# A new written-out order for an attention-plus-MLP kernel: 128 product sets instead of 137, and loads placed anew

## The chip, the cores and the metric

The kernel runs on one core of a Trainium2 chip. The metric is the device time of one execution in microseconds; runs are compared by their median.

## The reference, cut to what matters

Four batches of q, k and v, each 6080 x 256. Over the 6080 rows, the columns of q and k are normalised; the 256 x 256 scores go through a softmax; v is multiplied by the result; and the 24320 rows that come out go through a two-layer MLP with a tanh gelu and 2048 hidden units.

```python
qn = q / (np.linalg.norm(q, axis=1, keepdims=True) + 1e-06)
kn = k / (np.linalg.norm(k, axis=1, keepdims=True) + 1e-06)
s = kn.transpose(0, 2, 1) @ qn / tau          # 256 x 256 for each batch
a = np.exp(s - s.max(-1, keepdims=True))
a /= a.sum(-1, keepdims=True) + 1e-09
x = (v @ a).reshape(B * S, D)
h = x @ w_in
g = 0.5 * h * (1.0 + np.tanh(c * (h + 0.044715 * h * h * h)))
return g @ w_out
```

## The kernel before

**Stages.** The attention matrix is multiplied into `w_in` once for each batch (steps `aw.*`, `ac.*`), so the rest works directly on v. The 24320 tokens are cut into 25 blocks, mostly of 1024 tokens, six to a batch and seven in the last; a block is two halves of up to 512 tokens. Batch 0's scores are made first, from q and k in one go. The scores of batches 1, 2 and 3 are made in small pieces between the blocks of the batch before.

**A block's first product.** The hidden units are cut into 16 chunks of 128. A plain step `g.u` makes chunk u for both halves with 4 matmuls on TensorE (PE) into a pair of PSUM banks, and `G.u` is its gelu on ScalarE (ACT). A *set* i makes chunks i and 8+i together, in Strassen's manner (Winograd's form): 7 matmuls `m1.i` to `m7.i` instead of 8, on sums of weights (`SW`, tile `sw`) and of tokens (`vs`, tile `tv`, on VectorE, DVE), and in exchange copies and additions: on ACT `wcq` (L613), `wy5` (L616) and three gelus `wGq` (L626), `wGr` and `wGx` (L637), on DVE `wap` (L618) and `wax` (L621). `e` and `E` are block 0's product and gelu in another cut.

**The second product** goes in the same manner: `T1` to `T4` are sums on DVE (L704), `M1` to `M7` the matmuls, `y5`, `cq`, `ap`, `ax` the copies and additions. `c11` to `c22` transpose the result on DVE (L744) into one of three output buffers `ot`, and when a buffer is full four DMAs store it: from SP's queue, and for the last block but one two from SP's and two from POOL's. The last block uses `D` steps.

**Preparation.** `pA21`, `pA12`, `pNA` (ACT) and `pA11`, `pF0`, `pS3` and so on (DVE) make the eight forms of `w_out` from its float32 load `wst`.

**Loads.** `lq.c:b` and `lk.c:b` load a piece of q or k (384 KB, cast to bf16 on the way) from POOL's queue. `lv.h:n` casts half a block of v into bf16 in HBM, also from POOL's queue, and `lt.h:n` is a transposing load of it from SP's queue into `vT`, which has two buffers. POOL's loads wait for the last matmul that was recorded before them; `lt` has no such gate, it waits for its data, its buffer and the entries of SP's queue ahead of it:

```python
def load_vt(n, h):
    x, y = parts_of(n)[h]
    nc.sync.dma_start_transpose(out=vt_tile(n)[:, :, x:y], in_=v_bf.pop((n, h))[: y - x, :])
...
            elif what in ("lq", "lk"):
                load_one(n, *a, "qk".index(what[1]), GATE[0])
            elif what == "lv":
                cast_v(n, *a, GATE[0])
            elif what == "lt":
                load_vt(n, *a)
```

`qsq.c:b` and `ksq.c:b` square a piece (ACT at L158, or DVE at L160 for every other k), `f1` to `f3` fold the squares, `sp` and `sa` sum them, and `row.c_r:b` multiplies 128 of its rows into the 256 x 256 scores (L205). Of a piece, the square or the first `row` is the first use. `pow`, `kf`, `kr`, `krp`, `S`, `th`, `dn`, `rc`, `eT`, `rsum`, `rs` turn the scores into the softmax.

**The order.** Nothing is scheduled automatically. All work from the first `e` on is a string, `ORDER`, of some 3500 words, each `what.arguments@banks:block or batch`. They are recorded one after the other, and each engine runs its instructions in just this order, waiting at each one by semaphore for its inputs and for a free bank or buffer. PSUM banks are named by letters: `h` and `b` are the two pairs, `a`, `s`, `p`, `r` single banks; `m5.1:2` with `@b` means pair b.

```python
        for word in ORDER.split():
            run(word)
```

Of the kernel before, what the change touches and what calls it, by code (L numbers as in the profile page):

```python
# [954 lines left out]
row.0_0@r:1 m1.1@p:1 g.0@b:1 row.0_2@r:1 E.7_1:0 vs:1 lq.2:1 m5.1@h:1 M5.0@a:0 qsq.0:1 wcq.1:1 G.0:1
m6.1:1 f1.0:1 e.7_0@b:0 wy5.1:1 lk.2:1 wap.1:1 m2.1:1 row.0_5@r:1 row.0_4@r:1 row.0_3@r:1 m7.1:1
pA21:0 f2.0:1 SW.1:0 m3.1:1 E.7_0:0 y5:0 wGq.1:1 wax.1:1 g.8@b:1 row.1_4@r:1 T3.0:0 f3.0:1 lv.0:2
row.1_2@r:1 cq:0 m4.1:1 g.10@h:1 wGr.1:1 row.1_3@r:1 row.1_1@r:1 G.8:1 sp.0@p:1 lv.1:2 pS2:0 T2.0:0
T2.1:0 sa.0:1 M2.1:0 M2.0:0 ksq.1:1 qsq.1:1 g.2@b:1 G.10:1 f1.1:1 c11:0 lk.3:1 M6.0:0 f2.1:1
m1.5@p:1 M6.1:0 m5.5@h:1 ap:0 row.1_0@r:1 wcq.5:1 f3.1:1 G.2:1 wy5.5:1 lq.3:1 m2.5:1 m6.5:1  # L960
row.1_5@r:1 T3.1:0 wap.5:1 gc:1 g.3@b:1 M3.1:0 sp.1@r:1 ksq.2:1 lk.4:1 G.3:1 M7.0:0 m3.5:1 M3.0:0
g.11@b:1 T4.0:0 lt.1:2 qsq.2:1 wGq.5:1 lt.0:2 g.12@h:1 f1.2:1 sa.1:1 f2.2:1 M7.1:0 f3.2:1 c12:0
sp.2@r:1 ax:0 wGx.1:1 m7.5:1 G.11:1 m1.6@s:1 sa.2:1 wax.5:1 T4.1:0 G.12:1 g.4@b:1 row.2_1@r:1 lq.4:1
M4.0:0 T1.0:1 m5.6@h:1 row.3_2@r:1 row.3_4@r:1 qsq.3:1 wcq.6:1 G.4:1 m6.6:1 g.7@b:1 wy5.6:1 M4.1:0
wap.6:1 ksq.3:1 lq.5:1 row.3_5@r:1 T2.0:1 wGx.5:1 G.7:1 m4.5:1 m3.6:1 m2.6:1 m7.6:1 row.2_2@r:1
g.15@b:1 f1.3:1 f2.3:1 wax.6:1 wGq.6:1 wGr.5:1 lv.0:3 f3.3:1 c21:0 row.3_0@r:1 row.2_0@r:1 m4.6:1
G.15:1 sp.3@p:1 row.2_5@r:1 row.2_3@r:1 sa.3:1 vs:2 row.2_4@r:1 qsq.4:1 row.3_1@r:1 m1.1@a:2 g.0@h:2
m5.1@b:2 row.3_3@r:1 wcq.1:2 M1.1@p:1 lk.5:1 G.0:2 wy5.1:2 ksq.4:1 m6.1:2 T1.1:1 m2.1:2 wap.1:2
f1.4:1 g.3@h:2 wGx.6:1 wGr.6:1 m3.1:2 m7.1:2 M5.1@s:1 G.3:2 wax.1:2 f2.4:1 lk.6:1 g.8@h:2 f3.4:1
gc:1 wGq.1:2 T2.1:1 m4.1:2 M5.0@s:1 sp.4@r:1 M1.0@p:1 wGx.1:2 lv.1:3 G.8:2 y5:1 m5.2@b:2 sa.4:1  # L970
m1.2@r:2 c22:0 wGr.1:2 T3.0:1 cq:1 m1.5@a:2 m5.5@h:2 wcq.2:2 M2.1:1 m6.2:2 wcq.5:2 M2.0:1 m2.2:2
m6.5:2 wy5.2:2 wy5.5:2 ksq.5:1 T4.1:1 m2.5:2 wap.2:2 c11:1 wap.5:2 m3.2:2 lq.6:1 m7.2:2 wax.2:2
T4.0:1 M6.1:1 M6.0:1 m3.5:2 m4.2:2 wGq.2:2 qsq.5:1 lv.0:4 wGr.2:2 wGq.5:2 g.11@b:2 ap:1 m7.5:2
wGx.2:2 T3.1:1 wax.5:2 f1.5:1 M7.0:1 m1.6@r:2 M7.1:1 m5.6@h:2 G.11:2 lt.0:3 ax:1 f2.5:1 f3.5:1
m4.5:2 g.4@b:2 wcq.6:2 m6.6:2 wGr.5:2 M3.0:1 wy5.6:2 wGx.5:2 sp.5@a:1 M3.1:1 wap.6:2 sa.5:1 G.4:2
m1.7@a:2 m5.7@b:2 m7.6:2 qsq.6:1 ksq.6:1 M4.0:1 m3.6:2 m2.6:2 wcq.7:2 m6.7:2 wy5.7:2 lt.1:3 wax.6:2
m4.6:2 M4.1:1 wGq.6:2 wGx.6:2 f1.6:1 wap.7:2 lq.7:1 m7.7:2 m3.7:2 m2.7:2 f2.6:1 c12:1 g.12@h:2
wax.7:2 wGr.6:2 m1.1@p:3 wGq.7:2 c21:1 T1.0:2 wGx.7:2 row.5_3@r:1 G.12:2 m4.7:2 g.0@b:3 f3.6:1 vs:3
row.5_2@r:1 row.5_0@r:1 row.5_1@r:1 row.5_5@r:1 row.4_2@r:1 row.4_1@r:1 row.5_4@r:1 row.4_4@r:1
m5.1@h:3 wcq.1:3 m1.2@s:3 wGr.7:2 T1.1:2 row.4_3@r:1 G.0:3 sp.6@a:1 m6.1:3 wy5.1:3 m2.1:3  # L980
row.4_5@r:1 wap.1:3 m5.2@b:3 wcq.2:3 lk.7:1 m6.2:3 row.4_0@r:1 sa.6:1 qsq.7:1 m7.1:3 wy5.2:3
M5.1@a:2 m2.2:3 m3.1:3 wax.1:3 gc:1 m4.1:3 M5.0@a:2 wap.2:3 wGx.1:3 wGq.1:3 wGr.1:3 m1.3@r:3 m3.2:3
T3.0:2 m7.2:3 m5.3@h:3 wax.2:3 c22:1 T2.0:2 y5:2 wcq.3:3 wGq.2:3 M1.0@p:2 M1.1@p:2 m6.3:3 wy5.3:3
m4.2:3 T2.1:2 g.8@b:3 m2.3:3 wap.3:3 cq:2 M2.0:2 M2.1:2 ksq.7:1 lv.1:4 wGr.2:3 m3.3:3 m1.5@s:3
# [5 lines left out]
M4.1:2 g.0@h:4 m7.7:3 row.6_2@r:1 m3.7:3 c21:2 m2.7:3 row.7_3@r:1 G.0:4 m1.1@a:4 wax.7:3 m4.7:3  # L990
M3.1:2 M3.0:2 lq.0:2 lv.1:5 wGq.7:3 T1.0:3 vs:4 m5.1@h:4 wGr.7:3 wcq.1:4 c12:2 wy5.1:4 m1.2@s:4
m6.1:4 row.6_5@r:1 m2.1:4 m5.2@b:4 row.7_2@r:1 wap.1:4 wcq.2:4 T1.1:3 m1.3@p:4 row.6_1@r:1 m6.2:4
wGx.7:3 wy5.2:4 wap.2:4 m3.1:4 row.7_1@r:1 m2.2:4 m7.1:4 row.7_5@r:1 wGq.1:4 row.6_4@r:1 wax.1:4
m3.2:4 m7.2:4 row.6_0@r:1 row.7_0@r:1 row.6_3@r:1 row.7_4@r:1 m5.3@h:4 wcq.3:4 T2.1:3 wGq.2:4
wGx.1:4 m4.1:4 m6.3:4 gc:1 m5.4@b:4 m2.3:4 wy5.3:4 wGr.1:4 M5.0@r:3 wax.2:4 wap.3:4 m1.4@a:4 wy5.4:4
# [6 lines left out]
wax.6:4 M3.0:3 m5.7@h:4 m4.6:4 rc.0:1 ax:3 rc.3:1 wGq.6:4 wcq.7:4 c22:3 wGr.6:4 wy5.7:4 M4.0:3
m6.7:4 wap.7:4 M4.1:3 m2.7:4 lv.0:7 wGx.6:4 lq.1:2 m3.7:4 eT:1 m7.7:4 g.0@b:5 c21:3 wax.7:4 wGq.7:4
T1.1:4 G.0:5 rsum@a:1 aw.1@r:1 m4.7:4 g.4@h:5 vs:5 rs:1 M3.1:3 g.8@b:5 c12:3 G.4:5 wGr.7:4 T1.0:4
ac.1:1 m1.1@a:5 m5.1@h:5 aw.0@p:1 wcq.1:5 G.8:5 M5.1@s:4 aw.4@r:1 m6.1:5 wy5.1:5 wGx.7:4 ac.0:1
m2.1:5 m5.2@b:5 m1.2@p:5 wap.1:5 ac.4:1 M5.0@s:4 T2.1:4 m7.1:5 lk.1:2 m3.1:5 lv.1:7 wcq.2:5 y5:4
wy5.2:5 wGq.1:5 wax.1:5 m6.2:5 T3.1:4 M1.1@r:4 m4.1:5 wGr.1:5 M1.0@r:4 m2.2:5 lt.0:6 cq:4 wGx.1:5
wap.2:5 aw.5@a:1 T3.0:4 m7.2:5 g.12@h:5 m3.2:5 T2.0:4 wax.2:5 ac.5:1 wGq.2:5 lt.1:6 M2.1:4 m1.3@a:5
M2.0:4 m4.2:5 m5.3@b:5 wcq.3:5 wy5.3:5 wGx.2:5 wGr.2:5 G.12:5 T4.1:4 m6.3:5 M6.1:4 M6.0:4 c11:4
ksq.0:2 aw.2@p:1 wap.3:5 m7.3:5 m3.3:5 m2.3:5 ap:4 wax.3:5 M7.0:4 m5.5@h:5 ac.2:1 wGq.3:5 m4.3:5  # L1010
m1.5@p:5 M3.0:4 m5.6@b:5 wy5.5:5 wcq.5:5 M3.1:4 m6.5:5 lv.0:8 qsq.0:2 M7.1:4 wGr.3:5 SW.0:1 T4.0:4
c12:4 m1.6@a:5 wap.5:5 aw.3@r:1 ax:4 ac.3:1 wGx.3:5 wcq.6:5 m7.5:5 m3.5:5 m2.5:5 wGq.5:5 M4.0:4
f1.0:2 wy5.6:5 m6.6:5 wax.5:5 wap.6:5 m1.7@r:5 m5.7@h:5 M4.1:4 m2.6:5 m4.5:5 c21:4 m7.6:5 wcq.7:5
# [266 lines left out]
```

## Time and profile before

| | |
|---|---|
| median of three runs | 690.52 us (687.57 to 697.32) |
| the profiled execution's own time | 687.86 us |
| its span, first to last instruction | 686.1 us |
| mean granted TensorE clock | 0.999 |
| busy: PE, DVE, ACT | 97%, 92%, 91% of the span |
| matmuls | 3584 in the trace |
| DMA | 78.80 MB, mean 115 GB/s |
| transposing loads of v | 45, median 5.3 us from issue to landing, 3.1 to 12.4 |
| loads of k and of q (384 KB) | 21 each, median 5.6 and 5.2 us |

Busy times are unions of what an engine's instructions cover; matmuls overlap in them. "Idle before" is the time in which an engine had nothing to do, with the instruction or the DMA whose end released it. The chain of waits starts at the last instruction and goes back, at each step, to what released it.

### The profile page before, as it was taken

To read this page: it belongs to the slowest core of one execution; us is meant where nothing else is said; L and a number is where in the kernel's file an instruction comes from. 1 tells how busy PE (TensorE), PEld (TensorE's weight loads), DVE (VectorE), ACT (ScalarE), POOL (GpSimd) and SP (SyncE) were. 2 spreads that over 40 slices of the span, in tenths; PEclk is the share of its full clock that TensorE was granted. 3 is DMA by queue.
4 is the path that set the end of the run, shared out by engine and by line. 5 is a ranking of instruction groups with operands and counts; after the bars stand their busy time and mean duration, and the time that the engine had idled before them with its cause. 6 is when DMAs were issued, how large, how long until landed. Compare 5 with 4: busy or idle time off the path is not lost.

```text
span 686.1 us, 10286 instructions
## 1 busy us (share of the span) xinstructions
PE 665.7 (97%) x3584; PEld 337.1 (49%) x3584; DVE 629.1 (92%) x938; ACT 621.9 (91%) x941; POOL 74.2 (11%) x137
## 2 busy tenths in 40 slices
...
GB/s 240 207 251 158 124 171 114 102 143 74 142 103 118 167 114 98 100 96 93 103 105 142 142 157 138 84 53 108 79 135 62 91 75 61 72 83 90 76 32 89
DMA packets 161508, 78.80 MB, mean 115 GB/s; under 512 B 148512, under 2 KB 152224, under 8 KB 160736
## 3 DMA queue, kind: packets, MB, share of 16 engines
...
## 4 chain that ended last, share of the span: by engine, by line
PE 85%; DMA 7%; issue 4%; ACT 2%; POOL 1%; DVE 0%; DVEq 0%; POOLq 0%; ACTq 0%
PE p L482 22%; PE r L482 17%; PE rb L482 16%; PE qp L482 12%; PE h L482 10%; PE G L205 4%; DMA qk_g1b<-in_k_dram 3%; PE awp L374 2%; DMA qk_g1a<-in_q_dram 1%; DMA k<-in_k_dram 1%; DMA q<-in_q_dram 1%; ACT g L516 1%; PE e L482 1%; ACT g L637 0%; ACT qp L613 0%
## 5 line engine op out<-in xcount | busy, mean ns | idle before, releaser
L482 PEld LDWEIGHTS <-wcomb 128*128 128x128 bf16 x1408 | 136.5, 98 | 144.5 <-issue 1.7
L482 PE MATMUL p<-t,wcomb 128*128 128x512 bf16 (+2 forms) x576 | 142.8, 373 | 0.1
L482 PE MATMUL r<-g,wcomb 128*128 128x512 bf16 (+2 forms) x576 | 141.8, 373 | 0.0
L626 ACT ACTIVATE g<-qp 128x1024 bf16<-128x1024 f32 (+1 forms) x130 | 132.0, 1022 | 6.1 <-PE qp L482 5.9
L482 PEld LDWEIGHTS <-aw 128*128 128x128 bf16 x872 | 84.8, 98 | 94.8 <-issue 6.3
L704 DVE TENSOR_TENSOR t<-g,t 128x2048 bf16<-128x2048 bf16 (+2 forms) x96 | 112.8, 1182 | 0.0
L482 PE MATMUL rb<-tv,sw 128*128 128x512 bf16 (+3 forms) x288 | 101.4, 366 | 0.1
L618 DVE TENSOR_TENSOR qp<-rb,yw 128x512 f32<-128x512 f32 (+2 forms) x137 | 93.1, 686 | 8.7 <-ACT yw L616 4.8
L621 DVE TENSOR_TENSOR xw<-rb,yw 128x512 f32<-128x512 f32 (+2 forms) x137 | 92.6, 676 | 7.1 <-ACT g L637 3.4
L516 ACT ACTIVATE g<-h 128x1024 bf16<-128x1024 f32 (+1 forms) x92 | 94.1, 1032 | 1.8 <-PE h L482 1.4
L482 PE MATMUL h<-vT,aw 128*128 128x512 bf16 (+2 forms) x376 | 95.0, 377 | 0.6 <-ACT g L516 0.5
L616 ACT ACTIVATE yw<-qp 128x512 f32<-128x512 f32 (+2 forms) x137 | 80.8, 601 | 5.8 <-PE qp L482 4.1
L613 ACT ACTIVATE qp<-rb 128x512 f32<-128x512 f32 (+2 forms) x137 | 80.8, 595 | 4.7 <-PE rb L482 3.4
L637 ACT ACTIVATE g<-xw 128x512 bf16<-128x512 f32 (+1 forms) x130 | 82.1, 635 | 2.2 <-DVE xw L621 2.2
L482 PEld LDWEIGHTS <-sw 128*128 128x128 bf16 x576 | 56.2, 98 | 56.6 <-issue 0.6
L637 ACT ACTIVATE g<-rb 128x512 bf16<-128x512 f32 (+1 forms) x130 | 77.6, 602 | 1.9 <-PE rb L482 1.8
L704 DVE TENSOR_TENSOR t<-g 128x2048 bf16<-128x2048 bf16 (+2 forms) x48 | 56.5, 1181 | 0.7 <-ACT g L626 0.4
L704 DVE TENSOR_TENSOR g<-g,g 128x2048 bf16<-128x2048 bf16 (+2 forms) x48 | 56.6, 1183 | 0.0
L442 POOL DMA_DIRECT2D vb<-in_v_dram x45 | 22.5, 501 | 312.1 <-PE rb L482 199.4
L482 PE MATMUL rb<-tv,aw 128*128 128x512 bf16 (+3 forms) x144 | 50.9, 366 | 2.5 <-DVE xw L621 2.5
L482 PE MATMUL rb<-vT,aw 128*128 128x512 bf16 (+3 forms) x144 | 51.3, 366 | 0.0
L482 PE MATMUL qp<-vT,aw 128*128 128x512 bf16 (+3 forms) x144 | 51.3, 366 | 0.0
...
## 6 DMA issues: line engine op xcount, KB each, us to landing
out_dram<-ot SPq DMA_DIRECT2D x160, 128.0 KB, 3.1
...
```

The source lines that it names most:

```text
L205: nc.tensor.matmul(G[b][:, jc, :], lhsT=qt[:np_, r, jc * 128 : jc * 128 + 128], rhs=kt[:np_, r, :], start=first and jc == 0, stop=jc == 1, ...
L374: nc.tensor.matmul(ps, lhsT=ET[b][:, jc, ic * 128 : ic * 128 + 128], rhs=win_bf[:, jc, fs * 512 : fs * 512 + 512], start=jc == 0, stop=jc ...
L442: after(nc.gpsimd.dma_start(out=vb[: y - x, :], in_=v[b, t0 + x : t0 + y, :]), gate)
L482: GATE[0] = nc.tensor.matmul(*a, skip_group_check=True, **kw)
L516: nc.scalar.activation(g_half(n, u // 8)[:, u % 8].rearrange("p (t x) -> p t x", t=2), hp[:, :, :hc], AF.Gelu_apprx_tanh)
L613: apart(n, i, 0, "act", nc.scalar.activation(QP[n, i][:, 0, :w], RB[n, i][:, :w], AF.Copy))
L616: apart(n, i, 1, "act", nc.scalar.activation(YW[n, i][:, :w], QP[n, i][:, 1, :w], AF.Copy))
L618: apart(n, i, 1, "dve", nc.vector.tensor_add(QP[n, i][:, 1, :w], RB[n, i][:, :w], YW[n, i][:, :w]))
L621: nc.vector.tensor_add(XW[n, i][:, :w], RB[n, i][:, :w], YW.pop((n, i))[:, :w])
L626: nc.scalar.activation(g[:, k0].rearrange("p (t x) -> p t x", t=2), qp[:, :, :hc], AF.Gelu_apprx_tanh)
L637: nc.scalar.activation(g[:, k0, t], x[:, :w], AF.Gelu_apprx_tanh)
L704: nc.vector.tensor_sub(o, a, b)
```

## The change

Only `ORDER` changes. The functions, the tiles, the buffers and the steps before the first `e` are the same.

- Nine blocks have one set less and two plain steps more: blocks 3, 5, 9, 11, 15 and 17 have 5 sets and 6 plain steps (before: 6 and 4), blocks 4, 10 and 16 have 6 and 4 (before: 7 and 2). In all there are 128 sets and 112 plain steps, before 137 and 94.
- Every other step is there as before, and nearly all stand in another place. The words below show the start, the places around batch 3's last loads, and the end.

```diff
-e.0_0@h:0 aw.3@s:0 ac.3:0 aw.2@a:0 e.1_0@b:0 vp.1@r:0 ac.2:0 E.0_0:0 e.2_0@h:0 aw.4@p:0 E.1_0:0
-e.3_0@b:0 lv.1:1 lk.0:1 E.2_0:0 aw.5@s:0 vc.1_0:0 vc.1_1:0 E.3_0:0 e.3_1@h:0 aw.6@a:0 E.3_1:0
-e.0_1@b:0 E.0_1:0 ac.4:0 e.2_1@h:0 ac.5:0 SW.0:0 aw.7@r:0 pA11:0 e.1_1@b:0 E.2_1:0 ac.7:0 e.5_1@h:0
-vp.0@p:1 lq.0:1 E.1_1:0 E.5_1:0 e.4_1@b:0 T1.1:0 pF0:0 pS3:0 e.5_0@h:0 pA12:0 vc.0_1:1 ac.6:0
-E.4_1:0 M1.0@s:0 pF1:0 vc.0_0:1 e.4_0@b:0 lt.1:1 pS1:0 E.5_0:0 e.6_1@h:0 lq.1:1 pNA:0 E.4_0:0
...
-m4.6:14 lk.7:3 wGq.7:14 wax.7:14 m1.2@a:15 row.5_4@s:3 T1.0:14 g.0@b:15 m4.7:14 wGr.6:14 G.0:15
...
-m6.2:15 gc:3 wy5.1:15 wy5.2:15 wGx.7:14 wap.1:15 ksq.7:3 M5.1@p:14 m7.1:15 wap.2:15 wax.1:15
...
-m3.3:24 wGq.3:24 wGx.2:24 wGx.1:24 m7.3:24 D.2_1@r:24 D.2_0@s:24 D.6_0@s:24 D.0_0@s:24 c21:23 c22:23
...
+e.0_0@h:0 aw.3@s:0 aw.2@a:0 e.1_0@b:0 vp.1@r:0 E.0_0:0 E.1_0:0 lk.0:1 ac.2:0 aw.5@p:0 aw.4@a:0
+ac.3:0 e.2_0@h:0 vc.1_0:0 vc.1_1:0 e.2_1@b:0 E.2_0:0 lv.1:1 aw.6@s:0 e.3_0@h:0 aw.7@r:0 ac.4:0
+ac.5:0 E.2_1:0 pA21:0 E.3_0:0 e.3_1@b:0 SW.0:0 E.3_1:0 ac.6:0 e.0_1@h:0 E.0_1:0 e.1_1@b:0 vp.0@a:1
+E.1_1:0 ac.7:0 SW.1:0 lq.0:1 e.7_1@h:0 E.7_1:0 pS3:0 pF0:0 pA11:0 e.5_0@b:0 E.5_0:0 vc.0_0:1
+e.4_0@h:0 lt.1:1 m1.1@p:1 e.6_0@b:0 M1.0@s:0 E.4_0:0 lq.1:1 e.4_1@h:0 M1.1@s:0 pA12:0 E.6_0:0
...
+m1.7@r:14 G.4:14 ksq.6:3 m5.7@b:14 wGx.5:14 wap.6:14 wcq.7:14 wy5.7:14 lk.7:3 T1.0:14 row.4_4@s:3
...
+G.3:15 M2.1:14 wGx.1:15 ksq.7:3 T3.1:14 wap.2:15 M2.0:14 m4.1:15 m3.2:15 wGr.1:15 m7.2:15 g.11@b:15
...
+M3.0:23 M3.1:23 T4.1:23 m6.3:24 M4.0:23 M4.1:23 m2.3:24 D.5_1@a:24 wap.3:24 c21:23 m7.3:24 G.4:24
...
+D.5_0@r:24 D.6_0@r:24 D.2_1@a:24 c12:23 c22:23 D.7_0@r:24 D.3_0@r:24 D.3_1@a:24 D.4_1@a:24
...
```

More of the change, by code (lines that the diff above doesn't have):

```diff
@@ L955 @@
[L955 to L984, printed above, removed]
@@ L990 @@
[L990 to L995, printed above, removed]
@@ L1002 @@
[L1002 to L1013, printed above, removed]
@@ new lines @@
+lv.0:3 wGq.5:1 M7.1:0 M3.1:0 m4.5:1 m5.6@h:1 f1.2:1 wcq.6:1 m2.6:1 f2.2:1 G.15:1 m6.6:1 f3.2:1 ax:0
+c12:0 lq.4:1 wy5.6:1 M4.1:0 wap.6:1 sp.2@s:1 wGr.5:1 wGx.5:1 sa.2:1 M4.0:0 T1.0:1 m3.6:1 m7.6:1
+ksq.3:1 lk.4:1 wax.6:1 T2.0:1 g.7@b:1 wGq.6:1 G.7:1 qsq.3:1 row.3_3@p:1 m4.6:1 row.3_1@p:1
+row.2_2@p:1 row.3_5@p:1 g.4@h:1 row.3_4@p:1 row.3_2@p:1 row.2_1@p:1 m1.1@s:2 g.0@b:2 c21:0
+row.2_3@p:1 row.2_5@p:1 row.2_0@p:1 G.4:1 vs:2 lq.5:1 m5.1@h:2 wcq.1:2 G.0:2 wGr.6:1 wy5.1:2 f1.3:1
+f2.3:1 wGx.6:1 row.3_0@p:1 m2.1:2 T1.1:1 f3.3:1 row.2_4@p:1 m6.1:2 g.8@b:2 gc:1 sp.3@a:1 G.8:2
@@ new lines @@
+m6.2:4 m2.2:4 wax.1:4 wGr.7:3 wap.2:4 row.7_3@a:1 m4.1:4 M5.1@s:3 c22:2 m7.2:4 m3.2:4 gc:1 kf:1
+M5.0@s:3 m1.3@a:4 lv.0:7 wGq.1:4 wGx.1:4 wGr.1:4 wax.2:4 g.8@b:4 wGq.2:4 T2.0:3 m5.3@h:4 m4.2:4 y5:3
+wcq.3:4 m6.3:4 T3.0:3 M1.0@p:3 M1.1@p:3 wGx.2:4 wy5.3:4 wap.3:4 G.8:4 wGr.2:4 m3.3:4 m5.5@b:4 T2.1:3
+m7.3:4 m1.5@r:4 m2.3:4 cq:3 M6.0:3 kr:1 wcq.5:4 wax.3:4 m4.3:4 T4.1:3 m6.5:4 wy5.5:4 M2.1:3 m2.5:4
+wap.5:4 m3.5:4 wGr.3:4 krp@a:1 T4.0:3 S.1:1 T3.1:3 wGq.3:4 S.0:1 g.12@h:4 m7.5:4 M2.0:3 wGq.5:4
+wGx.3:4 G.12:4 wax.5:4 c11:3 M6.1:3 m1.6@a:4 lt.0:5 lt.1:5 ap:3 th.1:1 m5.6@b:4 th.0:1 m4.5:4 dn:1
@@ new lines @@
+m7.2:6 wGq.2:6 wGr.1:6 wGx.1:6 G.3:6 m1.5@r:6 M6.1:5 m5.5@b:6 wcq.5:6 wax.2:6 ap:5 wy5.5:6 g.11@h:6
+lk.4:2 G.11:6 m6.5:6 m4.2:6 wGx.2:6 wGr.2:6 wap.5:6 m2.5:6 c22:4 M3.1:5 m3.5:6 f2.0:2 m7.5:6
+m5.6@h:6 M7.1:5 wax.5:6 T4.1:5 wGq.5:6 m4.5:6 m1.6@s:6 g.4@b:6 f3.0:2 wy5.6:6 M3.0:5 wGr.5:6 wcq.6:6
+wGx.5:6 m1.7@r:6 lq.3:2 lv.0:9 m6.6:6 T4.0:5 G.4:6 c12:5 M7.0:5 sp.0@a:2 m5.7@b:6 wap.6:6 wcq.7:6
+wy5.7:6 m7.6:6 m6.7:6 m2.6:6 qsq.1:2 sa.0:2 row.1_4@a:2 m3.6:6 ax:5 wap.7:6 wax.6:6 M4.1:5 M4.0:5
+row.0_1@a:2 m7.7:6 row.1_3@a:2 row.0_0@a:2 c22:5 row.0_2@a:2 wGx.6:6 wGq.6:6 c21:5 wax.7:6 T1.0:6
@@ new lines @@
+f3.2:2 wGx.1:7 wy5.2:7 G.3:7 T3.0:6 sp.2@s:2 m6.2:7 sa.2:2 M2.1:6 wap.2:7 M6.1:6 c11:6 ap:6 m1.5@s:7
+m5.5@h:7 m3.2:7 m2.2:7 lt.0:8 m7.2:7 M3.1:6 T4.0:6 ksq.3:2 lt.1:8 lv.1:9 M7.0:6 wy5.5:7 lk.5:2
+wGq.2:7 wax.2:7 T3.1:6 wcq.5:7 qsq.3:2 g.11@b:7 M3.0:6 m6.5:7 T4.1:6 m4.2:7 M7.1:6 m2.5:7 c12:6
+G.11:7 wGx.2:7 wap.5:7 m1.6@r:7 wGr.2:7 m5.6@b:7 wcq.6:7 m3.5:7 ax:6 f1.3:2 wGq.5:7 m7.5:7 M4.0:6
+m1.7@a:7 m6.6:7 wy5.6:7 wax.5:7 wGx.5:7 g.4@h:7 lq.5:2 m4.5:7 G.4:7 wGr.5:7 lv.0:10 wap.6:7 f2.3:2
+f3.3:2 m2.6:7 m7.6:7 M4.1:6 T1.0:7 m5.7@h:7 m3.6:7 wax.6:7 wcq.7:7 c21:6 row.2_0@s:2 row.2_1@s:2
@@ new lines @@
+lt.0:9 wGr.1:8 m5.2@h:8 wcq.2:8 wGq.1:8 sp.4@r:2 M6.0:7 wy5.2:8 sa.4:2 c11:7 m6.2:8 qsq.5:2 wap.2:8
+M6.1:7 m1.5@r:8 m2.2:8 m3.2:8 m7.2:8 ap:7 m5.5@b:8 T4.0:7 wcq.5:8 wGq.2:8 M3.0:7 wy5.5:8 ksq.5:2
+m2.5:8 M3.1:7 g.11@h:8 m6.5:8 wax.2:8 lq.7:2 c22:6 c12:7 M7.1:7 m4.2:8 wGx.2:8 G.11:8 wap.5:8 f1.5:2
+wGr.2:8 m7.5:8 m1.6@p:8 m3.5:8 wax.5:8 f2.5:2 f3.5:2 m5.6@h:8 M7.0:7 wcq.6:8 wGq.5:8 m6.6:8 m4.5:8
+m2.6:8 wy5.6:8 ax:7 wGr.5:8 T4.1:7 row.5_3@s:2 g.4@b:8 wap.6:8 row.4_4@s:2 sp.5@r:2 wGx.5:8 sa.5:2
```

488 lines of the change are left out of this document (249 added, 239 removed).

## The prediction

> **What bounds the kernel now.** I read the page first, for the engine that is never free.
>
> ```profile
> PE 665.7 (97%) x3584; PEld 337.1 (49%) x3584; DVE 629.1 (92%) x938; ACT 621.9 (91%) x941; POOL 74.2 (11%) x137
> L626 ACT ACTIVATE g<-qp 128x1024 bf16<-128x1024 f32 (+1 forms) x130 | 132.0, 1022 | 6.1 <-PE qp L482 5.9
> L618 DVE TENSOR_TENSOR qp<-rb,yw 128x512 f32<-128x512 f32 (+2 forms) x137 | 93.1, 686 | 8.7 <-ACT yw L616 4.8
> L621 DVE TENSOR_TENSOR xw<-rb,yw 128x512 f32<-128x512 f32 (+2 forms) x137 | 92.6, 676 | 7.1 <-ACT g L637 3.4
> L516 ACT ACTIVATE g<-h 128x1024 bf16<-128x1024 f32 (+1 forms) x92 | 94.1, 1032 | 1.8 <-PE h L482 1.4
> L616 ACT ACTIVATE yw<-qp 128x512 f32<-128x512 f32 (+2 forms) x137 | 80.8, 601 | 5.8 <-PE qp L482 4.1
> L613 ACT ACTIVATE qp<-rb 128x512 f32<-128x512 f32 (+2 forms) x137 | 80.8, 595 | 4.7 <-PE rb L482 3.4
> L637 ACT ACTIVATE g<-xw 128x512 bf16<-128x512 f32 (+1 forms) x130 | 82.1, 635 | 2.2 <-DVE xw L621 2.2
> L637 ACT ACTIVATE g<-rb 128x512 bf16<-128x512 f32 (+1 forms) x130 | 77.6, 602 | 1.9 <-PE rb L482 1.8
> ```
>
> A busy matmul is drawn 373 ns long but they overlap, so 97% alone proves little. In the trace I took the time from one matmul's start to the next: 216 ns is the middle value for 512 columns, 202 for 480, 109 for 256, 96 for 224. The program's matmuls at these intervals come to 656.6 us. The first starts at 7.0 us and the last at 680.8, so PE stands still for about 17 us between, some 10 of them before 37 us, while the first q and k stream in (both orders have the same steps there). From the first `e` step (37.9 us) to the end only 7.2 us are lost. PE is the bound; DVE and ACT follow within 9%, but nearly never hold it up.
>
> Where those 7.2 us lie, the timeline around the largest tells (start, length, engine, line, and in brackets the idle time before), and then the chain of waits over the same window:
>
> ```profile
> 438.94 1.47 SPq L447 DMA_TRANSPOSE vT<-vb  x1
> 439.30 0.56 POOL L103 DMA_DIRECT2D k<-in_k_dram  x1 [6.66 <-PE rb L482]
> 448.36 1.58 ACT L158 ACTIVATE sq<-k 128x1280 bf16<-128x1280 bf16 x2 [2.90 <-DMA k<-in_k_dram]
> 450.48 0.69 DVE L621 TENSOR_TENSOR xw<-rb,yw 128x512 f32<-128x512 f32 x1 [2.62 <-ACT g L637]
> 451.23 0.38 PE L482 MATMUL rb<-tv,aw 128*128 128x512 bf16 x1 [2.49 <-DVE xw L621]
> ```
>
> ```profile
> 439.30 9.03 DMA k<-in_k_dram
> ```
>
> A transposing load of v goes out, a load of k 0.4 us after it; the k lands 9.03 us later. ACT stands at `ksq.7:3`, whose k is not there; the gelus queued behind it come late, DVE's add behind them, and PE misses its bank: 2.92 us in all (2.66 and 0.27). The same happened near 79 us: a q issued at 71.01 among two transposing loads landed after 7.71 us, and PE lost 0.67 and 0.26 us. So **3.9 us come from loads that land late**. Of the rest, 1.6 us are built in (float32 products of `krp`, 64-row pieces of `row`) or too small to place, and 1.7 us are short waits in crowded places, 0.53 of them at the first `e`, the other 1.2 for ACT.
>
> Of the 48 large q and k loads after 40 us, 24 had no transposing load in flight: they landed after 4.1 to 7.4 us, median 5.0. The other 24 took 4.3 to 12.4, and all nine above 7.4 are theirs.
>
> **The change, part by part.**
>
> *Nine sets become eighteen plain steps.* A set has 7 products, the two `g` steps 8. Six sets are in blocks of 512 columns a half, three of 480: 6 x 0.216 + 3 x 0.202 = 1.90 us; with two tiny filling products PE's sum is 658.5. **+1.9 us**, wholly on the bound engine. What goes away hides behind PE: on ACT 9 x (595 + 601 + 1022 + 602 + 635 - 2 x 1032) ns = 12.5 us, on DVE 9 x (686 + 676) = 12.3 us. I cost this relief at 0, because ACT and DVE already keep up; without that cover it would be the gain. It can loosen the crowded places by up to those 1.2 us.
>
> *Loads and their first uses.* PE is saturated, so a place in its order is a time: I added the intervals up from the first `e` in both orders and noted where each load's releasing matmul and its first reader stand. In the old order the distance is 5.8 us for `lq.7:1`, 6.1 for `lk.7:1`, 6.5 for `lq.7:3`, 6.1 for `lk.7:3`, 6.8 to 8.1 for five more: under the slow landings of 7.4 to 12.4 us. In the new order, from 58 us on, the shortest is 10.1 (`lk.3:1`); `lk.7:3` has 15.6. A transposing load starts when the buffer of two blocks earlier is free and the stores ahead of it on SP's queue are out; placing these the same way, from 58 us on none is issued within 2 us before a q or k load, and each has 10 us or more to its first reader. Even a 9.0 us landing is covered. **-3.9 us**; bounds 0 (the loads find something else to wait for) and -5.1 (the 1.2 us of waits for ACT go too).
>
> Against this stands the Trainium skill (DMA: Bandwidth & Descriptors, section Rules for kernel authors): it says that a transpose beside ordinary DMAs needs nothing, and its section on queues, rings and completion order that each DMA engine takes its queues in turns, a packet at a time. By that, moving them apart would be worth 0, and only the longer distances would help; the sum stays, since they cover the slow landings too. The trace's 12.4 against 7.4 us does not agree that company is free, though it can't tell sharing from blocking.
>
> *The first stage.* New here: `pA21` (1.07 us on ACT) stands ahead of `E.3_0`, and `aw.5`, `aw.4` ahead of `e.2_0`. In this stage PE needs a bank per `e` (0.86 us) and ACT frees it with a gelu each 0.92 to 1.0 us; old ACT had gaps of 0.3 us between them. Following the banks `h` and `b` by hand, `e.0_1` waits 0.7 to 0.95 us for `E.3_0`, and smaller waits follow: 1.2 to 2.0 us late by `g.0:1`, against 0.4 for the old order. **+1.0 us**; bounds 0 (the gaps absorb it) and +2.0.
>
> ```profile
> 42.02 1.02 ACT L536 ACTIVATE g<-e 128x1024 bf16<-128x1024 f32 x1 [0.29 <-PE e L482]
> 43.57 0.54 POOL L442 DMA_DIRECT2D vb<-in_v_dram  x1 [5.49 <-PE e L482]
> 44.10 0.58 POOL L103 DMA_DIRECT2D k<-in_k_dram  x1
> 49.97 1.32 SPq L447 DMA_TRANSPOSE vT<-vb  x1
> ```
>
> Also `lk.0:1` now precedes `lv.1:1` on POOL's queue. The two landed at 49.95 (v) and 51.78 (k); swapped, v lands near 51.8, its transposing load (5.0 us) near 56.8, not 54.97. `vs:1` stands at 55.2, so DVE waits some 1.5 us, which its 8% of idle time absorbs; `g.0:1`, the first matmul that reads it, stands at 57.4 plus the lateness of 1 us, 1.6 us behind the landing. Cost 0, with little cover.
>
> *The tail.* The last transposes to the output wait for a buffer that POOL's stores still read:
>
> ```profile
> 675.87 0.63 POOL L757 DMA_DIRECT2D out_dram<-ot  x1 [53.84 <-DVE ot L744]
> 677.03 4.00 PE L482 MATMUL o<-g,wcomb 128*128 128x224 bf16 x40
> 679.23 1.76 POOL L757 DMA_DIRECT2D out_dram<-ot  x3 [2.74 <-issue]
> 681.65 0.72 DVE L744 STREAM_TRANSPOSE ot<-o 128x224 f32<-128x224 f32 x2 [1.40 <-DMA out_dram<-ot]
> ```
>
> The step that fills that buffer, `c21:23`, moves from 5.9 to 6.8 us ahead of PE's end, so its stores end 1 us earlier: **-1.0 us** of the 1.4; bounds 0 and -1.4. `c22:23` moves later, but its stores have 5 us left.
>
> *Sum.* 686.1 + 1.9 - 3.9 + 1.0 - 1.0 = 684.1 us of span; with the 1.8 us around it in the profiled execution (687.9 - 686.1), 685.9. The three runs shown had a median of 690.5, 2.7 above the profiled execution. If that excess is loads landing later still, the new distances swallow most of it; I keep a quarter, 0.6: **686.5 us**.
>
> **The rivals.**
>
> *The load waits stay.* The distance was not the cause, or a queue slips: POOL issues loads in order, and one waiting for its buffer holds all behind. Then 685.9 + 3.9 = 689.8. Against it: at 448 us the landing and ACT's start are 0.03 us apart. The Trainium skill's rule, if it held alone, would lead here only as far as the distances fail.
>
> *Slower, by the first stage.* DMA is busiest there (the page's DMA digits are 9 in each of the first four slices), so a landing there slips easily. If block 1's transposed half lands 5 us later than I place it, 1.6 us of cover leave 3.4 us of PE wait; with the gelu chain at its upper bound (+1.0), 685.9 + 4.4 = 690.3, slower than the 687.9 it is compared with. It decides from a slip of 3.6 us on (1.6 of cover and the 2.0 by which I forecast less than before). Against it: the old load of the same kind landed in 5.0 us.
>
> *More goes.* ACT's relief removes the crowded waits, the tail wait goes whole and the first stage costs nothing: 686.1 + 1.9 - 5.1 - 1.4 + 1.8 = 683.3.
>
> *The order doesn't keep them apart.* PE's lateness shifts matmul-released loads but not those held by buffers; if pairs meet, a 9 to 12 us landing still fits into distances of 10 to 15 us nearly everywhere: within 1 us of the forecast, so no separate time.
>
> **How the numbers follow.** Forecast 60% (the case of meeting pairs included), load waits stay 18%, first stage slower 13%, more goes 9%. Range 682.5 to 693.5: below, the best case less 0.8; above, the slower rival's 690.3 with the 2.7 us by which the shown median lies over its profile, and 0.5 for late landings. A measurement here tells about 2% (13.8 us) from no change, as the runs from 687.6 to 697.3 suggest; every case lies within that. For faster by more, 676.7, PE would have to lose nothing and start earlier: 1%. For slower by more, 704, an unforeseen wait of 18 us: 3%.
>
> **What would show it.** Right: PE with 3592 matmuls and no wait over 1 us after 60 us; no `sq<-k` on ACT that waits for a DMA; ACT near 610 and DVE near 617 us busy; the last transposes not waiting on `out_dram`. The first-stage step is right if an `e` matmul waits for `g L536` near 46 us. Wrong: a wait of over 2 us on PE behind `sq` or `tv`, or a k or q load that lands after more than 8 us with its reader waiting.

## The result, and the profile after

The changed kernel takes 686.82 us (median of 22 runs, 686.43 to 686.91), the kernel before 690.30 us in the runs beside it (22 runs, 687.57 to 697.32): a ratio of 0.9939, 95% interval 0.9924 to 0.9955. That is 3.5 us less, and within the 2% of "no change". The profiled execution took 686.74 us with a span of 685.0, so between the two profiled executions only 1.1 us lie; the other 2.4 us of the median come from the runs of before, which spread over 10 us and lie, all but two, above their profile, while those of after lie within 0.5 us.

The page of the changed kernel: its engines, two groups that have fewer members now (130 and 137 before) and the plain gelu's, which has more (92 before), each with count, busy us, mean ns, and idle us before with what ended it:

```profile
PE 666.7 (97%) x3595; PEld 337.9 (49%) x3595; DVE 621.2 (91%) x920; ACT 613.8 (90%) x914; POOL 74.2 (11%) x137
...
L626 ACT ACTIVATE g<-qp 128x1024 bf16<-128x1024 f32 (+1 forms) x121 | 122.3, 1021 | 6.3 <-PE qp L482 5.6
L516 ACT ACTIVATE g<-h 128x1024 bf16<-128x1024 f32 (+1 forms) x110 | 111.8, 1023 | 7.5 <-PE h L482 6.9
...
L618 DVE TENSOR_TENSOR qp<-rb,yw 128x512 f32<-128x512 f32 (+2 forms) x128 | 87.4, 687 | 14.9 <-ACT yw L616 8.0
```

PE has 11 matmuls more in the trace (3584 before): nine for the sets and the two tiny filling products, where the prediction wrote 3592. ACT and DVE have some 8 us less each. The place near 440 us, from the timeline:

```profile
435.38 0.55 POOL L103 DMA_DIRECT2D k<-in_k_dram  x1 [6.60 <-PE qp L482]
...
440.73 1.33 SPq L447 DMA_TRANSPOSE vT<-vb  x1
...
450.83 1.59 ACT L158 ACTIVATE sq<-k 128x1280 bf16<-128x1280 bf16 x2
```

`lk.7:3` goes out with no transposing load beside it, lands after 4.48 us (9.03 before), and ACT reads it 15.4 us behind its issue, with no wait in brackets. The same holds everywhere: of the 48 large q and k loads after 40 us, 7 now have a transposing load in flight (24 before), and no reader waits. The first stage, and then the tail:

```profile
44.69 1.06 ACT L682 ACTIVATE wcomb<-wst 128x1024 bf16<-128x1024 f32 x1 [0.37 <-DMA wst<-in_moe_w_out_dram]
...
46.70 1.94 PE L482 MATMUL e<-vT,aw 128*128 128x512 bf16 x8 [0.91 <-ACT g L536]
```

```profile
673.71 0.63 POOL L757 DMA_DIRECT2D out_dram<-ot  x1 [81.90 <-DVE ot L744]
674.68 5.15 PE L482 MATMUL o<-g,wcomb 128*128 128x224 bf16 x52
677.06 1.77 POOL L757 DMA_DIRECT2D out_dram<-ot  x3 [2.72 <-issue]
...
679.87 0.71 DVE L744 STREAM_TRANSPOSE ot<-o 128x224 f32<-128x224 f32 x2 [0.43 <-PE o L482]
```

`pA21` (L682) holds ACT ahead of the gelu that `e` needs, and PE waits 0.91 us there; ACT itself had first waited 0.37 us for the load of `w_out` (`wst`). DVE's last transposes follow PE, and no longer wait for `out_dram` (1.40 us before).

Times from one matmul's start to the next, less the usual interval of its width, give this account of the two profiled executions (us):

| | before | after | difference |
|---|---|---|---|
| start of the first `e` | 37.91 | 37.40 | -0.51 |
| matmuls from there on, at their usual intervals | 635.69 | 637.62 | +1.93 |
| waits of PE for late loads | 3.85 | 0 | -3.85 |
| waits before 66 us (first stage) | 0.62 | 1.49 | +0.87 |
| all other waits, with those under 60 ns | 2.70 | 3.05 | +0.35 |
| PE's end to the last landing | 3.94 | 4.04 | +0.10 |

Not in it, and alike in both, are the last matmul itself and what follows the last landing, together 1.4 us. The first row is no effect of the order, which begins there: `e` starts between 37.4 and 37.9 us in the profiles of all these kernels.

### The profile page after: what moved, and what is told of

Its sections match the earlier page's. It is cut to its first block, busy times and chain, and to the rows that moved or that the text cites. A ratio compares the mean times of both kernels' runs of the same rounds, so it can differ in the third digit from the quotient of the medians.

```text
span 685.0 us, 10218 instructions
## 1 busy us (share of the span) xinstructions
PE 666.7 (97%) x3595; PEld 337.9 (49%) x3595; DVE 621.2 (91%) x920; ACT 613.8 (90%) x914; POOL 74.2 (11%) x137
## 4 chain that ended last, share of the span: by engine, by line
PE 94%; DMA 3%; DVE 1%; ACT 1%; issue 0%; SPq 0%; DVEq 0%; ACTq 0%
PE p L482 23%; PE r L482 17%; PE rb L482 16%; PE h L482 14%; PE qp L482 12%; PE G L205 6%; PE awp L374 2%; DMA qk_f<-in_q_dram 1%; DMA wst<-in_moe_w_out_dram 1%; PE e L482 1%; PE o L482 1%; PE ss L263 1%; PE warm L269 1%; DVE t L704 0%; PE ss L186 0%; ACT g L536 0%
## 5 line engine op out<-in xcount | busy, mean ns | idle before, releaser
L626 ACT ACTIVATE g<-qp 128x1024 bf16<-128x1024 f32 (+1 forms) x121 | 122.3, 1021 | 6.3 <-PE qp L482 5.6
L516 ACT ACTIVATE g<-h 128x1024 bf16<-128x1024 f32 (+1 forms) x110 | 111.8, 1023 | 7.5 <-PE h L482 6.9
L482 PE MATMUL h<-vT,aw 128*128 128x512 bf16 (+2 forms) x448 | 113.1, 376 | 0.0
L618 DVE TENSOR_TENSOR qp<-rb,yw 128x512 f32<-128x512 f32 (+2 forms) x128 | 87.4, 687 | 14.9 <-ACT yw L616 8.0
L482 PE MATMUL rb<-tv,sw 128*128 128x512 bf16 (+3 forms) x270 | 94.0, 366 | 0.0
L621 DVE TENSOR_TENSOR xw<-rb,yw 128x512 f32<-128x512 f32 (+2 forms) x128 | 86.3, 677 | 5.1 <-PE rb L482 2.1
L613 ACT ACTIVATE qp<-rb 128x512 f32<-128x512 f32 (+2 forms) x128 | 75.2, 592 | 8.1 <-PE rb L482 5.4
L637 ACT ACTIVATE g<-xw 128x512 bf16<-128x512 f32 (+1 forms) x121 | 75.8, 634 | 2.0 <-DVE xw L621 1.8
L482 PE MATMUL qp<-tv,sw 128*128 128x512 bf16 (+3 forms) x135 | 47.7, 366 | 0.0
L482 PE MATMUL qp<-vT,sw 128*128 128x512 bf16 (+3 forms) x135 | 47.6, 366 | 0.0
```

The source lines that it names most:

```text
L482: GATE[0] = nc.tensor.matmul(*a, skip_group_check=True, **kw)
L516: nc.scalar.activation(g_half(n, u // 8)[:, u % 8].rearrange("p (t x) -> p t x", t=2), hp[:, :, :hc], AF.Gelu_apprx_tanh)
L613: apart(n, i, 0, "act", nc.scalar.activation(QP[n, i][:, 0, :w], RB[n, i][:, :w], AF.Copy))
L618: apart(n, i, 1, "dve", nc.vector.tensor_add(QP[n, i][:, 1, :w], RB[n, i][:, :w], YW[n, i][:, :w]))
L621: nc.vector.tensor_add(XW[n, i][:, :w], RB[n, i][:, :w], YW.pop((n, i))[:, :w])
L626: nc.scalar.activation(g[:, k0].rearrange("p (t x) -> p t x", t=2), qp[:, :, :hc], AF.Gelu_apprx_tanh)
```

## The experiments

The theory: late loads made both the loss in the profiled run and the spread of the others; they are late where little distance meets a transposing load in flight. Rival 2: nine sets less on ACT and DVE loosened everything. Rival 3, a rule: a transposing load's company is harmless.

**All 137 sets, nine loads earlier.** The kernel before, with only these nine words moved (their new places; of the old ones only the first is shown, and `lk.7:3` takes the old place of `lq.7:3`); each load then stands 12 us or more ahead of its first use, and transposing loads stay where they were:

```diff
-wy5.5:1 lq.3:1 m2.5:1
+lk.3:1 lq.3:1 M6.0:0
+lk.4:1 lq.4:1 G.3:1
+lq.5:1 lk.5:1 row.3_5@r:1
+lv.1:3 lq.6:1 G.8:2
+lv.0:4 lq.7:1 wGr.2:2
+M4.1:1 lk.7:1 wGq.6:2
+M7.1:7 lk.7:2 m1.6@p:8
+lv.0:16 lq.7:3 g.3@h:14
+lk.7:3 M7.0:13
```

> The kernel before with all its 137 sets and every step in its old place, but for nine loads (lq.3:1, lq.4:1, lk.5:1, lq.6:1, lq.7:1, lk.7:1, lk.7:2, lq.7:3, lk.7:3), which go 2.4 to 9 us earlier, so that each is 12 us or more ahead of its first use. Transposing loads stay in company with some of them. Theory (late loads cost the 3.9 us of the profiled run, and cost more in the other runs, which makes them spread): no reader waits, span 686.1 - 3.9 = 682.2 (682.0 to 683.2), profiled execution 683.8 to 685, runs within 1 us of each other, median 684 to 685.2, which beats both kernels. Rival 2 (the relief of ACT and DVE by nine sets less did it): span 684.5 to 686.1 and runs that still spread over some us, median 688 to 690.5. Rival 3 (POOL's queue slips: an earlier load holds the casts of v behind it): a new wait for vT, over 687.

683.88 us (four runs, 683.73 to 684.00) against 691.3 for the kernel before beside it: ratio 0.9884, interval 0.9862 to 0.9907; span 681.9. From its page and its timeline:

```profile
PE 665.5 (98%) x3584; PEld 337.3 (49%) x3584; DVE 628.9 (92%) x938; ACT 621.5 (91%) x941; POOL 73.9 (11%) x137
```

```profile
419.80 5.05 SPq L447 DMA_TRANSPOSE vT<-vb  x2
...
422.75 0.55 POOL L103 DMA_DIRECT2D q<-in_q_dram  x1 [0.27 <-issue]
...
436.56 1.56 ACT L158 ACTIVATE sq<-q 128x1280 bf16<-128x1280 bf16 x2
```

All predicted here came: no PE wait over 0.35 us after 66 us, and no spread in these four runs, with ACT and DVE as full as before. Rival 2 falls. `lq.7:3`, issued here behind two transposing loads, landed after 9.88 us, and ACT read it 3.9 us later without a wait; a k at 197 us landed after 12.61, and nobody waited. In these runs distance alone was enough, without separation. This kernel is the fastest of all, with 2.9 us less than the changed one; in the profiled executions, from the first `e` to PE's end, 3.0 us, of which the changed one has 1.93 in more matmuls, 0.88 in its first stage and 0.2 in other waits.

**One cast later.** The kernel before, one word moved; the transposing load of block 16 then goes out at 454.7 and not beside `lk.7:3`, whose distance stays 6 us:

```diff
-wax.2:14 lv.0:16 g.3@h:14 ... ksq.7:3 M5.1@p:14
+wax.2:14 g.3@h:14 ... ksq.7:3 lv.0:16 M5.1@p:14
```

> The kernel before with one word moved: the cast lv.0:16 goes behind ksq.7:3, so that the transposing load lt.0:16 goes out some 8 us later, and none stands beside lk.7:3; its distance of 6 us to its reader is as it was. Theory: k lands after 4.1 to 5.8 us (9.03 before), ksq.7:3 doesn't wait, PE's 2.92 us near 449 us go: span 686.1 - 2.9 = 683.2 (682.9 to 684), the smaller waits near 80 us stay. Rival (the rule that company is harmless; the load was late for a reason of its own): it still lands after 8 to 9 us, span 686.1.

Locally as the theory says: the k landed after 4.40 us, and neither ACT nor PE waits near 450 us. But the span came to 689.0, and the median to 690.12 against 691.3 (ratio 0.9948, 0.9922 to 0.9975): in this execution the pair near 70 us went far worse than in the profile of before. ACT and PE in the timeline, then two stretches of time (busy us and count of PE, PEld, DVE, ACT and POOL, granted clock, DMA share, GB/s):

```profile
82.94 0.76 PE L205 MATMUL G<-k,q 128*128 128x256 bf16 x4 [2.85 <-DMA q<-in_q_dram]
85.02 0.58 PE L482 MATMUL rb<-tv,sw 128*128 128x512 bf16 x1 [1.32 <-ACT qp L613]
```

```profile
83.00 1.49 ACT L158 ACTIVATE sq<-q 128x1536 bf16<-128x1536 bf16 x1 [5.35 <-DMA q<-in_q_dram]
```

```profile
79.00:86.00 7.00, 2.48 (x12) 0.89 (x10) 2.14 (x2) 3.00 (x4) 0.53 (x1) 0.81 1.30 94
86.00:89.30 3.30, 3.30 (x8) 1.10 (x8) 2.84 (x4) 3.20 (x4) 0.00 (x0) 0.50 0.68 132
```

The q issued at 70.48 landed after 12.42 us, the k after it after 14.91 (7.71 and 7.80 before). The ten runs of this kernel lie from 684.56 to 690.89, three of them under 686: with the place near 440 mended, nearly the whole spread is still there.

**Two loads earlier.** The kernel before with only `lq.3:1` and `lq.4:1` moved, as above:

> The kernel before with only lq.3:1 and lq.4:1 moved, 2.4 and 6.2 us earlier, so that the pair near 80 us is read 12 and 13 us behind its place; the other seven, lk.7:3 with its 2.92 us of PE near 449 among them, stay. Theory (what spreads the runs of the kernel before over 686 to 694 us is the size of the collision near 70 to 90 us: two transposing loads and two loads): runs within 1.5 us of each other, median 686.5 to 688. Rival (the spread is the collision near 439 us, or many places together): runs still spread over 4 us or more, median 689 or above.

686.30 us (median of ten); nine of the runs lie from 686.03 to 687.82, against 687.04 to 693.49 of before beside them, and the ratio of these nine is 0.9928 (0.9906 to 0.9950). So **the spread of before was for the most part the pair near 70 to 90 us**, and two words take 4.6 us off the median; the other seven loads give the remaining 2.4. The tenth run, the profiled one, took 699.99 us: two transposing loads and two loads issued from 70.57 to 73.74 landed after 12.6 to 24.1 us.

```profile
97.92 1.48 ACT L158 ACTIVATE sq<-q 128x1536 bf16<-128x1536 bf16 x1 [11.69 <-DMA q<-in_q_dram]
96.67 0.58 PE L482 MATMUL rb<-vT,aw 128*128 128x512 bf16 x1 [10.05 <-DMA vT<-vb]
```

ACT waits for one of the two moved loads, and PE for a transposing load, issued at 72.49, which no word moved here. So twelve us of distance are no guarantee, and a transposing load has a distance of its own. The kernel with nine loads moved has the same order at this place; the ten runs shown with it, four above and six below, had no such case, which doesn't exclude one. In the changed kernel the two transposing loads meet one load there, at 71.51, which landed after 4.59 us; whether its 22 close runs owe more to this or to the distances, no run separates.

**Short distance without transposing loads.** The changed kernel, four loads moved later (the two casts follow so as not to hold `lk.7:3`):

```diff
-lq.4:1 ... lk.5:1 ... lk.7:2 ... lk.7:3 ... lv.1:16 ... lv.0:17
+row.2_0@p:1 lq.4:1 ... M2.1:1 lk.5:1 ... M1.0@a:8 lk.7:2 ... m6.1:15 lk.7:3 lv.1:16 lv.0:17
```

> The changed kernel with four loads of q and k brought back to about 6 us ahead of their first use (lq.4:1, lk.5:1, lk.7:2, lk.7:3; 5.8 to 6.4 us by PE's places, as in the kernel before), but with no transposing load of v going out within 2 us of them; the casts lv.1:16 and lv.0:17 stand behind lk.7:3. Theory (a load is late only where a transposing load is in flight beside it): they land after 4.1 to 6.0 us, readers wait 0 to 0.5 us in all, span 685.0 to 685.6, median 686.8 to 687.4. Rival 1 (the distance alone did it): readers wait as before the change, some 3 us on PE, median 689.5 or more. Rival 2 (the gain came from the relief of ACT and DVE by nine sets less, which loosens every wait): no change, 686.8.

689.15 us (688.75 to 689.57), 2.3 more than the changed kernel: between the two expectations. They landed after 5.07, 6.79, 6.25 and 4.59 us; three readers waited, as ACT's timeline shows at two places:

```profile
92.46 1.49 ACT L158 ACTIVATE sq<-q 128x1536 bf16<-128x1536 bf16 x1 [0.99 <-DMA q<-in_q_dram]
105.23 1.48 ACT L158 ACTIVATE sq<-k 128x1536 bf16<-128x1536 bf16 x1 [1.22 <-DMA k<-in_k_dram]
...
293.47 1.58 ACT L158 ACTIVATE sq<-k 128x1280 bf16<-128x1280 bf16 x2 [0.68 <-DMA k<-in_k_dram]
```

PE lost 0.88, 0.90 and 0.56 us there. The first, issued at 87.31 with stores in flight and another load 0.5 us behind it, was hardly late: ACT came to it after 4.2 us, not the 5.8 to 6.4 of PE's places, and a load by itself takes 4.4 to 4.8 (below). The second had a load 1.7 us before it, one 1.1 us behind it and then four stores, the third four stores between 0.3 us before it and 1.2 us behind it. The theory was too narrow: without a transposing load at its issue, loads and stores beside it made a load late by some 2 us, twice. The fourth, `lk.7:3`, with two casts 1.1 and 1.6 us behind it, was in time.

**And with one.** The same, and `lv.0:16` later too, so that the transposing load goes out with `lk.7:3`:

```diff
-lv.0:16 wax.1:14 ... m4.6:14 row.5_3@s:3
+wax.1:14 ... m4.6:14 lv.0:16 row.5_3@s:3
```

> The same as the kernel with four short distances, and one word more moved: the cast lv.0:16 goes later, so that the transposing load lt.0:16, which waits for it, goes out near 444.5 us, within 0.7 us of lk.7:3, whose reader stands 5.8 us behind its issue. Theory: k lands after 7.5 to 9.8 us (8 to 9 expected), ksq.7:3 on ACT waits 2.0 to 3.3 us for it, PE loses 1.5 to 3.0 us within the next 4 us; median 1.5 to 3.0 above the kernel without this move, so 688.3 to 690. Rival 2 (relief) and the rule that company is harmless: k lands after 4.1 to 6.0 us, median within 0.4 us of the other.

```profile
446.76 1.23 SPq L447 DMA_TRANSPOSE vT<-vb  x1
446.85 0.55 POOL L103 DMA_DIRECT2D k<-in_k_dram  x1 [4.14 <-PE rb L482]
...
452.88 1.59 ACT L158 ACTIVATE sq<-k 128x1280 bf16<-128x1280 bf16 x2
```

A miss: issued 0.09 us behind the transposing load, the k landed after 4.59 us as without it, its rest after 5.10, and nobody waited for it; 688.69 us (six runs, 688.40 to 691.14). The transposing load itself took 5.90 us instead of 3.47.

**The DMAs by themselves**, first in pairs and more, then in the groups that the trace shows, with engines at work beside them (`T` is `dma_start_transpose`, `k` and `q` the loads, `s` four stores, `c` a cast in HBM; each repetition starts when the last has landed):

```python
SERIES = k, T, T then k, k then T, T k T, s k T, c k, s k, k q          # the first, as they went out
GROUPS = {"Tk": T k rest, "sTk": s T k rest, "TqTk": T q T k}           # the second,
BACK = none, DVE, ACT, PE, all                                         # each with these
```

> DMAs by themselves, no attention and no MLP (only the moves are done): six repetitions each of a load of k or q (384 KB, cast), a transposing load of v (256 KB), both together with the load from 0 to about 2 us behind the transposing load or ahead of it, two transposing loads and a load, four stores and then both, a cast of v in HBM beside a load, four stores beside a load, and two loads. Theory (a transposing load that is already running slows a load that starts in it, and is slowed by it): alone 4 to 5 us and 3.1 to 3.7; load 0.3 to 1 us behind the transposing load 8 to 12 us, both ending within 0.3 us of each other, load issued ahead of it 4 to 6; with two transposing loads up to 15; beside a cast, stores or a second load 5 to 7. Rival (the engines share the queues fairly and company is harmless): every landing within 1.5 us of the one alone.

> DMAs by themselves again, now in three groups as the trace of the kernel before has them (a transposing load and a load 0.3 us behind it; four stores, a transposing load 2.1 us and a load 2.4 us behind their start, as near 439 us; two transposing loads and two loads, as near 70 us), each with nothing else running, with DVE adding, with ACT's gelus, with PE's matmuls, and with all three. Only these moves are done, not the attention or the MLP. Theory 1 (the makeup of the group decides): the group with stores lands its load after 8 to 10 us with nothing else running too, the group with two transposing loads after 8 to 15. Theory 2 (the engines beside them decide, by the memory they share with the DMAs): 4.8 to 7 us with nothing else running, 8 us or more with DVE or with all three. If every group lands within 7.5 us in every company, the pair's 9 to 15 us in the kernel come from something that neither has, and that stays open.

Landings in us, from the issue of each DMA:

| | load | transposing load |
|---|---|---|
| alone (6 each) | 4.35 to 4.77 | 3.05 to 3.38 |
| load 0.3 to 0.6 behind T | 4.81 to 5.27 | 5.29 to 5.98 |
| load 0.98 behind T | 5.29 to 5.81 | 3.10 to 3.30 |
| load 0.88 ahead of T | 4.39 to 4.71 | 4.54 to 4.83 |
| two T around the load | 5.70 to 6.72 | 3.07 to 7.38 |
| four stores, load with the last, T 0.55 behind it | 5.69 to 5.94 | 6.04 to 6.75 |
| beside a cast; four stores; a second load | 4.79 to 5.12; 6.32 to 6.62; 5.75 to 6.16 | |
| `Tk`, nothing beside; all engines | 4.24 to 4.53; 4.26 to 4.81 | 4.92 to 5.04; 5.03 to 5.51 |
| `sTk`, nothing; DVE; all engines | 6.11 to 7.47; 5.75 to 7.71; 5.04 to 8.35 | 7.06 to 8.38; 6.75 to 8.49; 6.62 to 8.77 |
| `TqTk`, nothing; all engines | 4.82 to 5.37; 4.88 to 5.83 | 4.97 to 5.80; 5.39 to 6.49 |

The theory's sizes fall: a pair costs the load 0.5 us, not 4, and the transposing load some 2.3. Stores in flight ahead of the pair matter more: near 439 us the kernel before had just this group, and 8.35 us of its 9.03 are reached, once in twenty repetitions. Four stores delay a load to 6.32 to 6.62 us with no transposing load too, if it goes out among them; what the transposing load adds is shown by the kernel with one cast later, whose k went out 1.2 us behind the last store, as in the kernel before, and landed after 4.40. Theory 2 of the second kernel falls too for the work tried: float32 additions from PSUM on DVE, gelus and matmuls change nothing; the sums of bf16 tiles that DVE does in the kernel were not tried. Company does a load little harm in a pair, and more among stores, a transposing load and a load together. The pair of pairs near 70 us, 4.8 to 6.8 us here, took 6.3 to 24 in the kernels with the order of before, where one or two loads issued 1.0 to 2.1 us ahead of it were still in flight, as in no group here: **what makes that stays open**.

**The changed kernel's two ends.** `pA21` behind `E.7_0`, and the first four stores of the last block from SP's and POOL's queues:

```diff
-ac.5:0 E.2_1:0 pA21:0 E.3_0:0 ... E.7_0:0
+ac.5:0 E.2_1:0 E.3_0:0 ... E.7_0:0 pA21:0
-            store(n, 1 if what == "sA" else 0, (nc.sync, nc.scalar, nc.sync, nc.scalar))
+            store(n, 1 if what == "sA" else 0, (nc.sync, nc.scalar if what == "sA" else nc.gpsimd) * 2)
```

> The changed kernel with two edits at its two ends. First stage: pA21 goes from ahead of E.3_0 to behind E.7_0. Theory (ACT's 1.07 us there are what e waits for): the 1.08 us of PE at 45.4 and most of the 0.41 at 50.4 go, up to 0.4 comes back later: 1.0 us less in the stretch before 66 us (0.8 to 1.5). Rival: aw.5 and aw.4 ahead of e.2_0, or banks, are the limit, and less than 0.4 us goes. Tail: of the last block's first four stores the two of ACT's queue go to POOL's, so that SP's last two stores no longer share a semaphore with a store that is still under way. Theory: they go out within 0.3 us of DVE's last transpose (1.13 us before), and the last landing comes 3.0 us behind PE's end instead of 4.04. Rival: POOL's queue is late with them, and the end stays. Sum by the theory: 686.8 - 2.0 = 684.8 median (684.3 to 685.6).

686.96 us: nothing gained at either end. ACT's and PE's timelines near 62 us:

```profile
61.25 1.06 ACT L682 ACTIVATE wcomb<-wst 128x1024 bf16<-128x1024 f32 x1
62.19 0.60 ACT L616 ACTIVATE yw<-qp 128x512 f32<-128x512 f32 x1
62.67 1.06 ACT L680 ACTIVATE wcomb<-wst 128x1024 bf16<-128x1024 f32 x1
```

```profile
46.93 0.81 PE L482 MATMUL e<-vT,aw 128*128 128x512 bf16 x3 [0.25 <-ACT g L536]
...
63.58 0.38 PE L482 MATMUL rb<-tv,sw 128*128 128x512 bf16 x1 [0.50 <-DVE qp L618]
```

The 1.08 us of PE near 45 us fell to 0.41, the 0.41 near 50 stayed, and 0.67 came back at 62.7, where `pA21` now delays `yw`, DVE's `qp` and the next matmul. So this move only shifts the wait. It need not cost that much: the order of before has the same three preparations on ACT in this stretch, at 49.9, 52.6 and 60.8 us, and loses 0.62 us in all. At the tail SP's last two stores went out 1.1 us nearer to PE's end, at 680.84 and 681.20, as the theory says, but the eight stores then landed after 1.67 to 2.70 us instead of 1.63 to 2.16, the last 3.90 us behind PE's end instead of 4.04. The wait was real and hid only the drain behind it.

**The fastest kernel, and the same tail.** The kernel with nine loads moved, the same line of stores edited, and `c21:23` earlier:

```diff
-wap.3:24 m3.3:24 ... D.0_0@s:24 c21:23 c22:23
+wap.3:24 c21:23 m3.3:24 ... D.0_0@s:24 c22:23
```

> The kernel before with all 137 sets, its nine loads 12 us or more ahead of their first use (this gave 683.9), and two edits at the tail: c21:23 stands 1.9 us earlier, behind wap.3:24, so that the last transposes need not wait for POOL's stores, and of the last block's first four stores two go from POOL's queue and not from ACT's. By the theory of the tail (a wait of 1.4 us on DVE, and behind it the wait for the semaphore of a store under way): the last landing comes 3.0 us behind PE's end instead of 3.9 to 4.0: 683.9 - 1.0 = 682.9 median (682.4 to 683.4). Rival (the stores of block 23 that now go out earlier meet others): no change, 683.9.

684.28 us (683.71 to 684.86), no gain: 683.73 to 684.00 without the tail's edits.

```profile
677.56 0.71 DVE L744 STREAM_TRANSPOSE ot<-o 128x224 f32<-128x224 f32 x2 [1.39 <-DMA out_dram<-ot]
```

The move of `c21:23` was empty: no step of DVE lies between its old place and its new one, so DVE did the same in the same order, and the wait of 1.4 us stayed. The stores from POOL's queue only made the end later: 4.70 us behind PE's end, 3.87 without.

## Why the prediction was right, and where it was not

The forecast of 686.5 us for a measured 686.82 rests on the right mechanism, and that it lies within 0.3 us is luck: for the profiled execution it said 685.9 (measured 686.74), and it added 0.6 for the spread (0.08 remained), two errors of opposite sign. Within the first, a tail 1.1 us worse than forecast and other waits 0.35 us longer were in part hidden by a start 0.51 us earlier, in which the order has no part. Point by point:

- **Work, +1.9.** Measured +1.93, all on PE. The relief of ACT and DVE, costed at 0, was worth 0: the kernel with all 137 sets and its loads moved has no more waits than the changed one. Its size was wrong, though: 8.1 us on ACT and 7.9 on DVE, where 12.5 and 12.3 were forecast (613.8 and 621.2 us busy, not 610 and 617). The forecast took lengths as drawn off a busy time in which they overlap: before, ACT's drawn lengths add up to 709 us, and its busy time is 622.
- **Loads, -3.9.** Measured -3.85, and the rivals "the load waits stay" and "slower by the first stage" did not come. That the long distances do it was shown by moving words alone; the separation is a second cover where distance is short (9.03 to 4.40 us near 440). The reason named, a transposing load beside a load, is too narrow: loads and stores beside a load made it late as well.
- **The Trainium skill's rule** (DMA: Bandwidth & Descriptors, section Rules for kernel authors), that a transpose next to ordinary DMAs needs nothing, stands in a row on transposes that spoil each other's data. It says nothing on time, so the prediction read too much into it. As a rule on time, company costs a load nearly nothing in a pair by itself (5.0 us, 4.5 alone) and in the kernel with 0.09 us between the two (4.59), and much where one word moved made 4.40 us of 9.03.
- **First stage, +1.0.** Measured +0.87, with the wait for `g L536` near 46 us as described. The extra cause named beside it, `aw.5` and `aw.4`, was not tried by itself. Block 1's half: v landed at 51.62 (placed at 51.8), its transposing load at 54.93 (placed at 56.8), and nobody waited.
- **The crowded waits,** held at 0 with a chance to lose 1.2: the other waits grew by 0.35; the largest of them, 0.36 us near 260 us, is for DVE's fold of squares. A lighter ACT and DVE did not shorten them.
- **Tail, -1.0: the step that failed.** The wait on `out_dram` went, as said; the end did not move (+0.10). The term took a wait on DVE for the path to the end. But without it DVE waits for PE's last products, and its last transposes end 0.75 us behind PE's end instead of 1.34, so 0.6 us were to be had and not 1.0; and behind them stand the last block's stores: SP's two waited 1.1 us for a semaphore that an earlier store still held, and without that wait the landings stretch.
- **The spread:** "the new distances swallow most of it" was right, and all but 0.5 us went; for the most part it was one place, near 70 to 90 us.
